# A retention layer and its mixture of adapters: scores between transposes, an interleaved tail, adapter weights from another queue

## The chip, the cores and the metric

The kernel runs on one core of a Trainium2 chip. The metric is the device time of one execution in microseconds (us); the median of three runs of the kernel before is 203.73 us (203.21 to 206.26). The engines are TensorE (PE; its weight loads are PEld), VectorE (DVE), ScalarE (ACT), GpSimd (POOL) and SyncE (SP), which here only issues transfers. Each engine works through its own list of instructions in order and waits on semaphores for the others. Transfers issued by any of them are moved by the core's 16 DMA engines.

## The reference

```python
# q, k, v: 8 batches x 8 heads x 576 positions x 64, float32
scores = q @ k.T / sqrt(64)
ret = (scores * gamma[h] ** (i - j) where i >= j, else 0) @ v
x = ret.transpose(0, 2, 1, 3).reshape(8 * 576, 512)      # 4608 tokens
logits = x @ w_gate                                      # 8 experts
w = softmax over the two largest logits of each token
out = x + sum over those two experts of w * ((x @ A[e]) @ B[e])   # rank 16
```

## The kernel before

**Tiling.** The 576 positions are four chunks of 128 and a tail of 64. The eight batches are two quads of four. A *unit* is one chunk and two batches of a quad: 16 full units, numbered 0 to 15, and after them two tail units, 16 and 17, each with four batches of 64 positions. Loads are made by chunk and quad: q, k and v are 1 MB each for a full chunk (`issue`, line 165), and three buffers of each are kept. A loop over the units (line 521) calls the stages in an order written out by hand; `mm`, `vec` and `act` (lines 80 to 87) chain the instructions of PE, DVE and ACT in exactly the order of the calls. GpSimd's and SyncE's instructions are not chained: a scheduler places them, from its own estimate of when their data will be there.

**Stages of a unit t.** `stage_T` transposes q and k on PE into PSUM (`pqT`, `pkT`), from where ACT copies them to `qT` and `kT`. `stage_S` computes scores (`ps`, in the tail `pe`) for its two batches; DVE multiplies them with the triangular mask into `rt` (`rh`). `stage_Q` adds the product of q and the running state `P` (`px`), `stage_U` computes the update of the state (`pu`, then `pn` on DVE and `P` on GpSimd), `stage_R` adds the product of masked scores and v to `px`, which DVE scales into `xT`. `stage_Z` multiplies `xT` with the adapter and gate weights (`AW`, result `pz`) and takes the two largest logits; `stage_W` makes the gate on ACT (`sg`) and DVE (`cm`) and scales the low-rank product (`zc`). `stage_B` transposes `xT` back into `po`, `stage_X` transposes `zc` (`pzt`, copied to `zT`), `stage_Y` adds the product of `zT` and `Bcat` to `po`, has ACT copy it to `osb`, and issues the stores. Stages W, B, X and Y of a unit run during the next one. All PSUM tiles share eight buffers (`pp`).

**The start.** Units 0 and 1 go through T, S, Q, U, R and Z together at t = 0, with idle matmuls (`spin`) ahead of each operand's first transposes. v must be scaled by GpSimd (`scale_v`, line 214) before pu and px may read it, in place, two instructions a unit. The adapter weights are four transfers of 64 KB and the gate weights one of 16 KB, all from SyncE (`load_moe`, line 150), between the loads of the first and of the second quad; GpSimd then copies `AW[0]` to `AW[1]` with the halves of the partitions exchanged (line 537).

**The tail.** Unit 16 takes batches 0 to 3 and unit 17 batches 4 to 7; their loads are issued apart, each with two halves per operand. The stores of a tail unit are four of 64 rows.

Of the kernel before, what the change touches and what calls it, by code (L numbers as in the profile page):

```python
# [10 lines left out]
FP32 = mybir.dt.float32  # L11
# [7 lines left out]
def kernel(  # L19
# [129 lines left out]

    def load_moe():  # L150
        for dt in range(HP):
            nc.sync.dma_start(
                out=AW[0][:, dt, 0:ER].rearrange("p (e r) -> p e r", e=E),
                in_=moe_A[:, 128 * dt : 128 * dt + 128, :].rearrange("e d r -> d e r"),
            )
        nc.sync.dma_start(
            out=AW[0][:, :, ER : ER + E],
            in_=moe_w_gate.rearrange("(t p) e -> p t e", p=128),
        )
        nc.gpsimd.dma_start(out=Bcat, in_=moe_B.rearrange("e r d -> (e r) d"))  # L160


    nat = {}

    def issue(n):
        if n >= len(quads):
            return
        c, qd = quads[n]
        first = n == 0
        tl = [  # L170
            iop.tile([128, QUAD, H, Dh], FP32, tag=tag, name=tag) for tag in ("q32", "k32", "v32")
        ]
        if c == NFULL:
            for src, dst in zip((q, k, v), tl):
                for g in range(2):
                    nc.sync.dma_start(
                        out=dst[64 * g : 64 * g + 64, 0:2].rearrange("p s h d -> p (s h) d"),
                        in_=src[
                            QUAD * qd + 2 * g : QUAD * qd + 2 * g + 2, :, C * c : C * c + L, :
                        ].rearrange("s h j d -> j (s h) d"),  # L180
                    )
        def load(n, lo, hi):
            nc.sync.dma_start(  # L183
                out=tl[n][:, lo:hi].rearrange("p b h d -> p (b h) d"),
                in_=(q, k, v)[n][
                    QUAD * qd + lo : QUAD * qd + hi, :, C * c : C * c + C, :
                ].rearrange("b h j d -> j (b h) d"),
            )

        if first:  # L190
            for n in range(3):
                load(n, 0, 4)
                if n == 1:
                    nc.sync.dma_start(out=pack, in_=dr_pack.ap())  # L194
            load_moe()
        elif c < NFULL:
            for n in range(3):
                load(n, 0, 4)
        for sl in range(2):
            nat[(c, qd, sl)] = [x[:, 2 * sl : 2 * sl + 2] for x in tl]  # L200
# [20 lines left out]
                op=ALU.mult,  # L221
            )

    def stage_T(t, pause=0):

        q32, k32, v32 = nat[units[t]]
        s = st.setdefault(t, {})
        for src, nm in ((q32, "qT"), (k32, "kT")):
            if nm == "kT":
                spin(pause)  # L230
            dst = s[nm] = wk.tile([128, 2, HP, C], FP32, tag=nm, name=nm)
            ps = [pp.tile([128, HP, 2, L], FP32, tag="pb", name=f"p{nm}") for _ in range(2)]
            for hp in range(HP):
# [20 lines left out]
    def stage_Q(t):  # L254
# [8 lines left out]
        for hp in range(HP):  # L263
            for y in range(1 if full else 2):
                for ho in range(2):
                    for x in range(2):
                        Pt = P[2 * qd + sl][:, :, x] if full else P[2 * qd + x][:, :, y]
                        i = slice(0, C) if full else rows(y)
                        mm(
                            px[x][rows(ho ^ x), hp, i],  # L270
                            lhsT=Pt[rows(ho), hp, :],
                            rhs=s["qT"][rows(ho), x, hp, i],
                            start=(hp == 0 and y == 0),
                            stop=False,
                            skip_group_check=True,
                        )

    def stage_S(t):
        s = st[t]
        rt = s.setdefault("rt", {})  # L280
        if not is_full(t):
# [20 lines left out]
                )  # L302
                rt[ho] = r
            return
        for b in range(2):
            ps = [pp.tile([128, HP, C], FP32, tag="pb", name=f"ps{ho}") for ho in range(2)]
            for hp in range(HP):
                for ho in range(2):
# [102 lines left out]
                    )  # L411
        s["po"] = po

    def stage_X(t):
        s = st[t]
        pzt = pp.tile([128, 2, 128], FP16, tag="pb", name="pzt")
        for g in range(2):
            mm(
                pzt[:, g, :], lhsT=s["zc"][:, g, :], rhs=ident16,
                is_transpose=True, start=True, stop=True,  # L420
            )
        zt = mo.tile([128, 2, 128], FP16, tag="zT", name="zT")
        act("copy", out=zt, in_=pzt)
        s["zT"] = zt

    def stage_Z(t):
        s = st[t]
        pz = pp.tile([128, 2, ER + E], FP32, tag="pb", name="pz")
        for g in range(2):
            for dt in range(HP):  # L430
                mm(
                    pz[:, g, :],
                    lhsT=s["xT"][g][:, dt, :],
                    rhs=AW[g][:, dt, :],
                    start=(dt == 0),
                    stop=(dt == HP - 1),
                    skip_group_check=True,
                )
        m8 = mo.tile([128, 2, E], FP32, tag="m8", name="m8")
        ns = mo.tile([128, 2], FP32, tag="ns", name="ns")  # L440
        sg = mo.tile([128, 2, E], FP32, tag="sg", name="sg")
        cm = mo.tile([128, 2, E], FP32, tag="cm", name="cm")
        lg = mo.tile([128, 2, E], FP32, tag="lg", name="lg")
        vec("tensor_copy", out=lg, in_=pz[:, :, ER : ER + E])
        for g in range(2):
            vec("max", out=m8[:, g, :], in_=lg[:, g, :])
        vec("scalar_tensor_tensor", 
            out=ns, in0=m8[:, :, 0], scalar=-1.0, in1=m8[:, :, 1],
            op0=ALU.mult, op1=ALU.subtract,
        )  # L450
        s["route"] = lg, m8, ns, sg, cm, pz

    def stage_W(t):
        s = st[t]
        lg, m8, ns, sg, cm, pz = s.pop("route")
        for g in range(2):
            act("activation", 
                out=sg[:, g, :], in_=lg[:, g, :], func=AFT.Sigmoid,
                bias=ns[:, g : g + 1], scale=2.0,
            )  # L460
        for g in range(2):
            vec("scalar_tensor_tensor", 
                out=cm[:, g, :], in0=lg[:, g, :], scalar=m8[:, g, 1:2], in1=sg[:, g, :],
                op0=ALU.is_ge, op1=ALU.mult,
            )
        zc = mo.tile([128, 2, ER], FP16, tag="zc", name="zc")
        for g in range(2):
            vec("tensor_tensor", 
                out=zc[:, g, :].rearrange("p (e r) -> p e r", e=E),
                in0=pz[:, g, 0:ER].rearrange("p (e r) -> p e r", e=E),  # L470
                in1=cm[:, g, :].unsqueeze(2).broadcast_to((128, E, R)),
                op=ALU.mult,
            )
        s["zc"] = zc

    def stage_Y(t):
        c, qd, sl = units[t]
        s = st.pop(t)
        po = s["po"]
        osb = outp.tile([128, 2, HP, 2, Dh], FP32, tag="osb", name="osb")  # L480
        bv = Bcat.rearrange("p (a o d) -> p a o d", a=HP, o=2)
        for cc in range(2):
            for g in range(2):
                mm(
                    po[cc][:, g, :, :],
                    lhsT=s["zT"][:, g, :],
                    rhs=bv[:, :, cc ^ g, :],
                    start=False,
                    stop=True,
                    skip_group_check=True,  # L490
                )
        for cc in range(2):
            for g in range(2):
                act("copy", out=osb[:, g, :, cc ^ g, :], in_=po[cc][:, g])
        of = osb.rearrange("p g a o d -> p g (a o d)")
        for g in range(2):
            for x in range(1 if c < NFULL else 2):
                bt = 2 * sl + g if c < NFULL else 2 * g + x
                n0 = S * (QUAD * qd + bt) + C * c
                if c < NFULL:  # L500
                    nc.sync.dma_start(out=out[n0 : n0 + C, :], in_=of[:, g, :])
                else:
                    nc.sync.dma_start(out=out[n0 : n0 + L, :], in_=of[rows(x), g, :])

    issue(0)
    issue(1)
# [14 lines left out]
    for t in range(NU):  # L521
# [3 lines left out]
            scale_v(t + 1)  # L525
        if t == 0:
            spin(12)
            stage_T(0, pause=12)
            stage_T(1)
            stage_S(0)  # L530
            stage_S(1)
            for u in range(2):
# [2 lines left out]
                stage_R(u)  # L535
            for ho in range(2):
                gp.tensor_copy(out=AW[1][rows(ho)], in_=AW[0][rows(1 - ho)])
            for u in range(2):
                stage_Z(u)
            stage_T(2)  # L540
            continue
        if t == 1:
            continue
        done = [0, 1] if t == 2 else [t - 1] if t > 2 else []
        if not is_full(t):
            stage_Q(t)
        stage_S(t)
        for u in done:
            stage_W(u)
        if t + 1 < NU:  # L550
            stage_T(t + 1)
        for u in done:
            stage_B(u)
        if is_full(t):
            stage_Q(t)
        stage_U(t)
        stage_R(t)
        for u in done:
            stage_X(u)
        stage_Z(t)  # L560
        for u in done:
            stage_Y(u)
    stage_W(NU - 1)
    stage_B(NU - 1)
    stage_X(NU - 1)
    stage_Y(NU - 1)
    return

# [28 lines left out]
```

## Time and profile before

| | |
|---|---|
| median of three runs | 203.73 us |
| the profiled execution | 203.81 us |
| its span, first to last instruction | 202.1 us |
| PE busy | 184.5 us, 91% of the span |
| DVE, ACT, POOL busy | 109.4, 71.5, 58.3 us |
| bytes moved | 38.73 MB, mean 192 GB/s |

Times inside the span count from its first instruction. Busy time of PE is that of matmuls which overlap each other, so it tells where PE had work, not how near it is to its peak. A line of the timeline reads: start, length, engine, line of the kernel, operation, output and inputs, shapes, number of instructions, and in brackets how long the engine stood idle before and what released it. PE, DVE and ACT instructions bear the line of the helper that records them (81, 84, 87), so they are told apart by their tiles.

### The profile page before, as it was taken

To read this page: it belongs to the slowest core of one execution; us is meant where nothing else is said; L and a number is where in the kernel's file an instruction comes from. 1 tells how busy PE (TensorE), PEld (TensorE's weight loads), DVE (VectorE), ACT (ScalarE), POOL (GpSimd) and SP (SyncE) were. 2 spreads that over 40 slices of the span, in tenths; PEclk is the share of its full clock that TensorE was granted. 3 is DMA by queue.
4 is the path that set the end of the run, shared out by engine and by line. 5 is a ranking of instruction groups with operands and counts; after the bars stand their busy time and mean duration, and the time that the engine had idled before them with its cause. 6 is when DMAs were issued, how large, how long until landed. Compare 5 with 4: busy or idle time off the path is not lost.

```text
span 202.1 us, 8056 instructions
## 1 busy us (share of the span) xinstructions
PE 184.5 (91%) x3588; PEld 164.6 (81%) x3588; DVE 109.4 (54%) x270; ACT 71.5 (35%) x196; POOL 58.3 (29%) x68
## 2 busy tenths in 40 slices
PE   7889977999999999999999999899999999989740
PEld 2378966899999999999999999799999999978620
DVE  0249628648647565757555655646464646363420
ACT  2040054163525252525243434234343434343060
POOL 5059108043046203636203722610502060200000
PEclk9999999999999999999999999999999999999995
DMA  4996999999999949952989798439145702022044
GB/s 122 312 241 90 296 275 246 284 276 254 322 310 270 289 175 272 274 181 109 250 245 303 247 257 267 111 88 255 51 135 122 194 11 100 3 107 99 11 104 104
DMA packets 47698, 38.73 MB, mean 192 GB/s; under 512 B 18352, under 2 KB 43056, under 8 KB 47664
## 3 DMA queue, kind: packets, MB, share of 16 engines
q1 hardware_dynamic: 47520, 38.09, 66.0%
q8 instruction: 28, 0.46, 1.0%
q0 software_dynamic: 144, 0.13, 0.4%
q14 instruction: 6, 0.05, 0.1%
HBM read 28.91 MB, written 9.44 MB: 190 GB/s over the span
## 4 chain that ended last, share of the span: by engine, by line
PE 79%; DVE 7%; SPq 4%; DMA 3%; ACT 2%; POOL 1%; issue 1%; ACTq 0%; POOLq 0%
PE px L81 22%; PE pz L81 17%; PE ps L81 13%; PE po L81 9%; PE pu L81 9%; PE pkT L81 3%; PE pqT L81 3%; DMA v<-in_v_dram 3%; DVE rt L84 2%; SPq L183 2%; DVE cm L84 2%; SPq L194 2%; PE pzt L81 2%; POOL v L217 1%; ACT osb L87 1%
## 5 line engine op out<-in xcount | busy, mean ns | idle before, releaser
L84 DVE TENSOR_TENSOR rt<-ps,tri 128x512 f32<-128x512 f32 x64 | 39.6, 682 | 13.4 <-PE ps L81 13.4
L217 POOL TENSOR_TENSOR v<-v,pack 128x512 f32<-128x512 f32 x36 | 36.5, 1043 | 23.7 <-DMA v<-in_v_dram 23.7
L349 POOL TENSOR_TENSOR P<-pn,gdec 128x512 f32<-128x512 f32 x12 | 15.3, 1273 | 82.2 <-DVE pn L84 82.2
L81 PE MATMUL pz<-AW,xT 128*128 128x136 f32 x288 | 37.2, 283 | 1.1 <-DVE xT L84 1.1
L81 PEld LDWEIGHTS pz<-AW,xT 128*128 128x128 f32 x288 | 34.5, 190 | 1.6 <-DVE xT L84 1.6
L81 PE MATMUL ps<-qT,kT 64*128 64x128 f32 x512 | 32.6, 278 | 1.6 <-ACT kT L87 1.4
L81 PEld LDWEIGHTS ps<-qT,kT 64*128 64x128 f32 x512 | 29.7, 188 | 4.6 <-PE po L81 2.7
L87 ACT COPY osb<-po 128x256 f32<-128x256 f32 x72 | 21.5, 389 | 30.0 <-PE po L81 28.2
L81 PE MATMUL px<-rt,v 128*64 128x128 f32 x512 | 30.8, 273 | 0.0
L84 DVE TENSOR_TENSOR xT<-px,asc 128x512 f32<-128x512 f32 x36 | 24.7, 691 | 7.3 <-PE px L81 6.0
L87 ACT COPY qT<-pqT 128x512 f32<-128x512 f32 x32 | 17.2, 590 | 31.3 <-PE pqT L81 31.3
L81 PEld LDWEIGHTS px<-rt,v 128*64 128x64 f32 x512 | 27.8, 137 | 0.0
L87 ACT COPY zT<-pzt 128x256 f16<-128x256 f16 x18 | 6.6, 373 | 53.8 <-PE pzt L81 53.8
L87 ACT COPY kT<-pkT 128x512 f32<-128x512 f32 x36 | 19.6, 608 | 9.7 <-PE pkT L81 9.7
L81 PE MATMUL pu<-v,k 128*64 128x64 f32 x512 | 18.6, 225 | 1.4 <-DVE zc L84 1.0
L81 PEld LDWEIGHTS pu<-v,k 128*64 128x64 f32 x512 | 16.4, 138 | 3.9 <-issue 3.1
L84 DVE TENSOR_TENSOR pn<-pu,P 128x512 f32<-128x512 f32 x12 | 8.3, 691 | 20.4 <-PE pu L81 20.4
L81 PE MATMUL po<-id,xT 64*128 64x64 f32 x288 | 15.7, 229 | 2.2 <-DVE zc L84 1.6
L84 DVE COPY lg<-pz 128x16 f32<-128x16 f32 x18 | 3.1, 174 | 25.8 <-PE pz L81 25.8
L81 PEld LDWEIGHTS po<-id,xT 64*128 64x128 f32 x288 | 12.1, 139 | 4.4 <-DVE rt L84 2.4
L81 PE MATMUL px<-qT,P 64*64 64x128 f32 (+1 forms) x512 | 15.6, 262 | 0.0
L81 PEld LDWEIGHTS px<-qT,P 64*64 64x64 f32 x512 | 12.5, 133 | 1.3 <-issue 0.4
(42 smaller groups left out, 147.3 us busy)
## 6 DMA issues: line engine op xcount, KB each, us to landing
out_dram<-osb SPq DMA_DIRECT2D x32, 256.0 KB, 3.3
q<-in_q_dram SPq DMA_DIRECT2D x4, 256.0 KB, 4.4
k<-in_k_dram SPq DMA_DIRECT2D x4, 256.0 KB, 3.7
v<-in_v_dram SPq DMA_DIRECT2D x4, 256.0 KB, 4.0
out_dram<-osb SPq DMA_DIRECT2D x8, 128.0 KB, 2.3
AW<-in_moe_A_dram SPq DMA_DIRECT2D x4, 64.0 KB, 3.5
q<-in_q_dram SPq DMA_DIRECT2D x8, 0.2 KB, 6.3
k<-in_k_dram SPq DMA_DIRECT2D x8, 0.2 KB, 9.1
```

The costliest lines, as they stand in the source:

```text
L81: chain("pe", nc.tensor.matmul(*args, **kw))
L84: chain("dve", getattr(nc.vector, fn)(**kw))
L87: chain("act", getattr(nc.scalar, fn)(**kw))
L183: nc.sync.dma_start(out=tl[n][:, lo:hi].rearrange("p b h d -> p (b h) d"), in_=(q, k, v)[n][QUAD * qd + lo : QUAD * qd + hi, :, C * c : C ...
L194: nc.sync.dma_start(out=pack, in_=dr_pack.ap())
L217: nc.gpsimd.tensor_tensor(out=vv[:, b], in0=vv[:, b], in1=gv[:, 0 if is_full(t) else 1].unsqueeze(2).broadcast_to((128, H, Dh)), op=ALU.mult,)
L349: nc.gpsimd.tensor_tensor(out=Pt, in0=pn, in1=gdec, op=ALU.mult)
```

## The change

- In the loop over full units, the scores of the first batch come first, then the transposes of the next unit's q, then the scores of the second batch, then the transposes of k. The gate's sigmoid is a stage of its own (`stage_V`), called between the first scores and q's transposes.
- Of units 0 and 1, both q are transposed ahead of both k, with 10 instead of 12 idle matmuls between. Unit 0's W, B, X and Y move into t = 0.
- `load_moe` issues its five transfers from ScalarE's queue, after the copies of unit 0's kT; the transfer of `Bcat` stays on GpSimd's.
- Units 16 and 17 are interleaved: 17's state product, scores and products with v are placed among the routing stages of 16, and 17 itself routes and stores its two halves one after the other. The second PSUM tile of those halves is copied out by DVE.
- A tail unit takes two batches of each quad; both units' tail loads are issued together, as six transfers of 512 KB instead of twelve of 256 KB, and a tail store is one of two batches of 64 rows.

The stages X, Z, W and Y take the halves to work on as an argument `gs`; their instructions for a whole unit are the same as before. In the built program, the order of GpSimd's first instructions after `asc` is: the two copies of AW, then the scaling of v. SyncE's first loads are q, k, the constants, v, and then at once q, k and v of the second and third quads.

```diff
     def load_moe():
         for dt in range(HP):
-            nc.sync.dma_start(
+            act(
+                "dma_start",
                 out=AW[0][:, dt, 0:ER].rearrange("p (e r) -> p e r", e=E),
                 in_=moe_A[:, 128 * dt : 128 * dt + 128, :].rearrange("e d r -> d e r"),
             )
...
         if c == NFULL:
+            if qd > 0:
+                return
             for src, dst in zip((q, k, v), tl):
                 for g in range(2):
                     nc.sync.dma_start(
-                        out=dst[64 * g : 64 * g + 64, 0:2].rearrange("p s h d -> p (s h) d"),
-                        in_=src[
-                            QUAD * qd + 2 * g : QUAD * qd + 2 * g + 2, :, C * c : C * c + L, :
-                        ].rearrange("s h j d -> j (s h) d"),
+                        out=dst[64 * g : 64 * g + 64].rearrange("p s h d -> p (s h) d"),
+                        in_=src[HALF * g : HALF * g + HALF, :, C * c : C * c + L, :].rearrange(
+                            "s h j d -> j (s h) d"
+                        ),
                     )
...
         for cc in range(2):
-            for g in range(2):
-                act("copy", out=osb[:, g, :, cc ^ g, :], in_=po[cc][:, g])
+            for g in gs:
+                if spread and cc == 1:
+                    vec("tensor_copy", out=osb[:, g, :, cc ^ g, :], in_=po[cc][:, g])
+                else:
+                    act("copy", out=osb[:, g, :, cc ^ g, :], in_=po[cc][:, g])
...
+            bt = HALF * g + 2 * qd
+            nc.sync.dma_start(
+                out=out.rearrange("(b s) d -> b s d", b=B)[bt : bt + 2, C * c : C * c + L, :],
+                in_=of[:, g, :],
+            )
...
         if t == 0:
             spin(12)
-            stage_T(0, pause=12)
-            stage_T(1)
+            stage_T(0, ("qT",))
+            stage_T(1, ("qT",))
+            spin(10)
+            stage_T(0, ("kT",))
+            load_moe()
+            stage_T(1, ("kT",))
             stage_S(0)
             stage_S(1)
...
-            for u in range(2):
-                stage_Z(u)
-            stage_T(2)
+            stage_Z(0)
+            stage_W(0)
+            stage_T(2, ("qT",))
+            stage_Z(1)
+            stage_T(2, ("kT",))
+            stage_B(0)
+            stage_X(0)
+            stage_Y(0)
             continue
...
+        if t == NU - 1:
+            break
+        if is_full(t):
+            stage_S(t, (0,))
+            stage_V(t - 1)
+            stage_T(t + 1, ("qT",))
+            stage_S(t, (1,))
+            stage_W(t - 1)
+            stage_T(t + 1, ("kT",))
+            stage_B(t - 1)
+            stage_Q(t)
+            stage_U(t)
+            stage_R(t)
+            stage_X(t - 1)
+            stage_Z(t)
+            stage_Y(t - 1)
+            continue
+
+        stage_Q(t)
         stage_S(t)
+        stage_W(t - 1)
+        stage_T(t + 1)
+        stage_B(t - 1)
         stage_R(t)
+        stage_Q(t + 1)
+        stage_X(t - 1)
         stage_Z(t)
+        stage_W(t)
+        stage_Y(t - 1)
+        stage_S(t + 1)
+        stage_B(t)
+        stage_X(t)
+        stage_R(t + 1)
+        stage_Y(t)
+        for g in range(2):
+            stage_Z(t + 1, (g,))
+            stage_W(t + 1, (g,))
+        stage_B(t + 1)
+        for g in range(2):
+            stage_X(t + 1, (g,))
+            stage_Y(t + 1, (g,), spread=True)
```

More of the change, by code (lines that the diff above doesn't have):

```diff
@@ L155, in load_moe @@
             )
-        nc.sync.dma_start(
+        act(
+            "dma_start",
             out=AW[0][:, :, ER : ER + E],
@@ L163 @@
     nat = {}
+    HALF = B // 2
+    assert HALF == QUAD
     def issue(n):
@@ L176, in issue @@
                     nc.sync.dma_start(
-                        out=dst[64 * g : 64 * g + 64, 0:2].rearrange("p s h d -> p (s h) d"),
-                        in_=src[
-                            QUAD * qd + 2 * g : QUAD * qd + 2 * g + 2, :, C * c : C * c + L, :
-                        ].rearrange("s h j d -> j (s h) d"),
-                    )
+                        out=dst[64 * g : 64 * g + 64].rearrange("p s h d -> p (s h) d"),
+                        in_=src[HALF * g : HALF * g + HALF, :, C * c : C * c + L, :].rearrange(
+                            "s h j d -> j (s h) d"
+                        ),
+                    )
+            for u in range(2):
+                nat[(c, u, 0)] = [x[:, 2 * u : 2 * u + 2] for x in tl]
+            return
         def load(n, lo, hi):
@@ L194, in issue @@
                     nc.sync.dma_start(out=pack, in_=dr_pack.ap())
-            load_moe()
         elif c < NFULL:
@@ L222, in scale_v, with stage_T @@
             )
-    def stage_T(t, pause=0):
-        q32, k32, v32 = nat[units[t]]
+    def stage_T(t, names=("qT", "kT")):
         s = st.setdefault(t, {})
-        for src, nm in ((q32, "qT"), (k32, "kT")):
-            if nm == "kT":
-                spin(pause)
+        for nm in names:
+            src = nat[units[t]][0 if nm == "qT" else 1]
             dst = s[nm] = wk.tile([128, 2, HP, C], FP32, tag=nm, name=nm)
@@ L266, in stage_Q @@
                     for x in range(2):
-                        Pt = P[2 * qd + sl][:, :, x] if full else P[2 * qd + x][:, :, y]
+                        Pt = P[2 * qd + sl][:, :, x] if full else P[2 * x + qd][:, :, y]
                         i = slice(0, C) if full else rows(y)
@@ L276, in stage_Q, with stage_S @@
                         )
-    def stage_S(t):
+    def stage_S(t, bs=(0, 1)):
         s = st[t]
@@ L304, in stage_S @@
             return
-        for b in range(2):
+        for b in bs:
             ps = [pp.tile([128, HP, C], FP32, tag="pb", name=f"ps{ho}") for ho in range(2)]
@@ L412, in stage_B, with stage_X, stage_Z @@
         s["po"] = po
-    def stage_X(t):
+    BOTH = (0, 1)
+    def stage_X(t, gs=BOTH):
         s = st[t]
-        pzt = pp.tile([128, 2, 128], FP16, tag="pb", name="pzt")
-        for g in range(2):
+        n = len(gs)
+        pzt = pp.tile([128, n, 128], FP16, tag="pb", name="pzt")
+        for y, g in enumerate(gs):
             mm(
-                pzt[:, g, :], lhsT=s["zc"][:, g, :], rhs=ident16,
+                pzt[:, y, :], lhsT=s["zc"][g], rhs=ident16,
                 is_transpose=True, start=True, stop=True,
             )
-        zt = mo.tile([128, 2, 128], FP16, tag="zT", name="zT")
+        zt = mo.tile([128, n, 128], FP16, tag=f"zT{n}", name="zT")
         act("copy", out=zt, in_=pzt)
-        s["zT"] = zt
-    def stage_Z(t):
+        for y, g in enumerate(gs):
+            s.setdefault("zT", {})[g] = zt[:, y, :]
+    def stage_Z(t, gs=BOTH):
         s = st[t]
-        pz = pp.tile([128, 2, ER + E], FP32, tag="pb", name="pz")
-        for g in range(2):
+        n = len(gs)
+        pz = pp.tile([128, n, ER + E], FP32, tag="pb", name="pz")
+        for y, g in enumerate(gs):
             for dt in range(HP):
                 mm(
-                    pz[:, g, :],
+                    pz[:, y, :],
                     lhsT=s["xT"][g][:, dt, :],
@@ L438, in stage_Z @@
                 )
[L439 to L443, printed above, removed]
+        m8 = mo.tile([128, n, E], FP32, tag=f"m8{n}", name="m8")
+        ns = mo.tile([128, n], FP32, tag=f"ns{n}", name="ns")
+        lg = mo.tile([128, n, E], FP32, tag=f"lg{n}", name="lg")
         vec("tensor_copy", out=lg, in_=pz[:, :, ER : ER + E])
-        for g in range(2):
-            vec("max", out=m8[:, g, :], in_=lg[:, g, :])
-        vec("scalar_tensor_tensor",
+        for y in range(n):
+            vec("max", out=m8[:, y, :], in_=lg[:, y, :])
+        vec(
+            "scalar_tensor_tensor",
             out=ns, in0=m8[:, :, 0], scalar=-1.0, in1=m8[:, :, 1],
@@ L450, in stage_Z, with stage_V @@
         )
-        s["route"] = lg, m8, ns, sg, cm, pz
-    def stage_W(t):
+        s[("route", gs)] = lg, m8, ns, pz
+    def stage_V(t, gs=BOTH):
         s = st[t]
[L455 to L459, printed above, removed]
-            )
-        for g in range(2):
-            vec("scalar_tensor_tensor",
-                out=cm[:, g, :], in0=lg[:, g, :], scalar=m8[:, g, 1:2], in1=sg[:, g, :],
+        n = len(gs)
+        lg, m8, ns, pz = s[("route", gs)]
+        sg = mo.tile([128, n, E], FP32, tag=f"sg{n}", name="sg")
+        for y in range(n):
+            act(
+                "activation",
+                out=sg[:, y, :], in_=lg[:, y, :], func=AFT.Sigmoid,
+                bias=ns[:, y : y + 1], scale=2.0,
+            )
+        s[("route", gs)] += (sg,)
@@ L464, in stage_W @@
+    def stage_W(t, gs=BOTH):
+        s = st[t]
+        n = len(gs)
+        if len(s[("route", gs)]) == 4:
+            stage_V(t, gs)
+        lg, m8, ns, pz, sg = s.pop(("route", gs))
+        cm = mo.tile([128, n, E], FP32, tag=f"cm{n}", name="cm")
+        zc = mo.tile([128, n, ER], FP16, tag=f"zc{n}", name="zc")
+        for y in range(n):
+            vec(
+                "scalar_tensor_tensor",
+                out=cm[:, y, :], in0=lg[:, y, :], scalar=m8[:, y, 1:2], in1=sg[:, y, :],
                 op0=ALU.is_ge, op1=ALU.mult,
@@ L465, in stage_W @@
             )
[L466 to L471, printed above, removed]
+        for y, g in enumerate(gs):
+            vec(
+                "tensor_tensor",
+                out=zc[:, y, :].rearrange("p (e r) -> p e r", e=E),
+                in0=pz[:, y, 0:ER].rearrange("p (e r) -> p e r", e=E),
+                in1=cm[:, y, :].unsqueeze(2).broadcast_to((128, E, R)),
@@ L472, in stage_W, with stage_Y @@
                 op=ALU.mult,
             )
-        s["zc"] = zc
-    def stage_Y(t):
+            s.setdefault("zc", {})[g] = zc[:, y, :]
+    def stage_Y(t, gs=BOTH, spread=False):
         c, qd, sl = units[t]
-        s = st.pop(t)
+        s = st[t]
         po = s["po"]
-        osb = outp.tile([128, 2, HP, 2, Dh], FP32, tag="osb", name="osb")
+        if gs[0] == 0:
+            s["osb"] = outp.tile([128, 2, HP, 2, Dh], FP32, tag="osb", name="osb")
+        osb = s["osb"]
         bv = Bcat.rearrange("p (a o d) -> p a o d", a=HP, o=2)
@@ L482, in stage_Y @@
         for cc in range(2):
-            for g in range(2):
+            for g in gs:
                 mm(
                     po[cc][:, g, :, :],
-                    lhsT=s["zT"][:, g, :],
+                    lhsT=s["zT"][g],
                     rhs=bv[:, :, cc ^ g, :],
@@ L492, in stage_Y @@
         for cc in range(2):
-            for g in range(2):
-                act("copy", out=osb[:, g, :, cc ^ g, :], in_=po[cc][:, g])
-        of = osb.rearrange("p g a o d -> p g (a o d)")
[L496 to L503, printed above, removed]
+            for g in gs:
+                if spread and cc == 1:
+                    vec("tensor_copy", out=osb[:, g, :, cc ^ g, :], in_=po[cc][:, g])
+                else:
+                    act("copy", out=osb[:, g, :, cc ^ g, :], in_=po[cc][:, g])
+        of = osb.rearrange("p g a o d -> p g (a o d)")
+        for g in gs:
+            if c < NFULL:
+                n0 = S * (QUAD * qd + 2 * sl + g) + C * c
+                nc.sync.dma_start(out=out[n0 : n0 + C, :], in_=of[:, g, :])
+                continue
[4 more added lines that the diff above has]
+            )
     issue(0)
@@ L543 @@
             continue
-        done = [0, 1] if t == 2 else [t - 1] if t > 2 else []
-        if not is_full(t):
-            stage_Q(t)
-        stage_S(t)
[L548 to L556, printed above, removed]
+        if t == NU - 1:
[8 more added lines that the diff above has]
+            stage_B(t - 1)
+            stage_Q(t)
+            stage_U(t)
[3 more added lines that the diff above has]
+            stage_Y(t - 1)
+            continue
+        stage_Q(t)
+        stage_S(t)
+        stage_W(t - 1)
+        stage_T(t + 1)
+        stage_B(t - 1)
         stage_R(t)
-        for u in done:
-            stage_X(u)
+        stage_Q(t + 1)
+        stage_X(t - 1)
         stage_Z(t)
[L561 to L566, printed above, removed]
+        stage_W(t)
[12 more added lines that the diff above has]
+            stage_Y(t + 1, (g,), spread=True)
     return
```

## The prediction

> **What bounds the kernel now.** I read the page's totals first, then the chain that ended last, then the start of the run on GpSimd and SyncE, then the stores.
>
> ```profile
> span 202.1 us, 8056 instructions
> PE 184.5 (91%) x3588; PEld 164.6 (81%) x3588; DVE 109.4 (54%) x270; ACT 71.5 (35%) x196; POOL 58.3 (29%) x68
> PE   7889977999999999999999999899999999989740
> ```
>
> TensorE is the bound: its row is at 9 from the eighth slice to almost the end. A full unit repeats every 10.2 us (scores start at 72.10, 82.30, 92.50) with no gap, so an exchange inside that loop moves little. Only the two ends have room. The chain:
>
> ```profile
> 15.57 2.06 POOL v L217 x2
> 17.67 1.04 PE pu L81 x28
> ...
> 28.67 1.10 ACT kT L87 x2
> ...
> 33.49 1.87 DVE cm L84 x2
> ...
> 42.47 1.99 PE ps L81 x32
> ```
>
> The reader is to see that GpSimd's scaling of v releases the first pu, that two later waits (for kT and for cm) cost some 3 us, and that unit 3's scores start at 42.47. I measure the start of the run by that moment. GpSimd and SyncE in order of time:
>
> ```profile
> 15.57 4.05 POOL L217 TENSOR_TENSOR v<-v,pack 128x512 f32<-128x512 f32 x4 [1.15 <-DMA v<-in_v_dram]
> 19.68 1.32 POOL L537 COPY AW<-AW 64x544 f32<-64x544 f32 x2
> ...
> 10.18 6.37 SPq L152 DMA_DIRECT2D AW<-in_moe_A_dram  x4
> 16.60 0.59 SPq L156 DMA_DIRECT2D AW<-in_moe_w_gate_dram  x1
> ```
>
> GpSimd scales v first and copies the adapter weights (AW) second. The end:
>
> ```profile
> 194.38 0.43 PE L81 MATMUL pzt<-ident,zc 128*128 128x128 f16 x2 [1.32 <-DVE zc L84]
> ...
> 195.80 1.20 ACT L87 COPY osb<-po 128x256 f32<-128x256 f32 x4 [0.53 <-PE po L81]
> ...
> out_dram<-osb SPq DMA_DIRECT2D x32, 256.0 KB, 3.3
> out_dram<-osb SPq DMA_DIRECT2D x8, 128.0 KB, 2.3
> ```
>
> The last matmul ends at 195.9, the last copy at 197.0, the last store lands near 200.9, and 1.2 us later the span ends.
>
> **What the Trainium skill says.** (1) "DMA: Bandwidth & Descriptors", section Queues, rings and completion order: each DMA engine serves the queues in turn and switches only at a packet's end. The trace agrees, and shows how long a turn is. Bcat (GpSimd's queue, issued at 2.72) began on each engine only when that engine had finished its whole share of the 1 MB q load (ends 6.08 to 6.64), although k, issued at 2.21, was waiting too; k followed. A turn was a whole transfer. (2) The same page, section Why a DMA increments its semaphore by 16 and not by 1: a transfer runs on the largest number of engines, at most 16, that divides the outermost dimension of both sides; a smaller number takes the lowest-numbered engines. Every store of before has 128 or 64 there. While stores run, some 95 packets of 2 KB start per 0.5 us at 84 ns each: 95 x 84 = 8.0 us of work in 0.5 us, 16 engines. A smaller number is in no trace of before. (3) "TensorE: Matmul & The Clock Gate", Part 1: after some 3.4 us without work the clock halves until it has been busy as long. The trace agrees: the first twelve spin matmuls took 5.30 us, the second twelve 2.76, and the clock is 0.50 from 199 us on. (4) "SBUF — State Buffer", section Who interferes with whom: a VectorE instruction with two SBUF inputs waits for a GpSimd instruction that reads SBUF. Agreed: a pair of cm takes 0.35 us alone and 1.95 at 33.41, inside GpSimd's scaling.
>
> **The change part by part.** In the built order of the changed kernel GpSimd's two AW copies stand *ahead* of the first scaling of v. So the first pu waits until all five AW transfers have landed.
>
> *When AW lands.* The issues stand on ScalarE behind the first two kT copies, which end at 12.00 + 2.09/2 = 13.05. Before, a first packet followed an issue by some 1.4 us (q: 17.39 to 18.8), so AW is ready near 14.5, as v ends on the engines (14.5 to 15.2). SyncE now goes straight to the next q, k and v. By packets: an AW transfer is 64 per engine at 11 ns, 0.7 us; a load is 64 at 54 ns, 3.5 us; the gate weights 32 at 9 ns, 0.3. One turn each: AW 15.6, q 19.1, AW 19.8, k 23.3, AW 24.0, v 27.5, AW 28.2, next q 31.7, gate 32.0, landed about 33. The bounds are 19 (where it landed before, issued from SyncE alone) and 36 (first turn missed). I take 33.
>
> *What follows.* AW copies 1.32 to 34.3; two scalings 2.06 to 36.4; the rest of pu 1.0 to 37.4. TensorE then runs px, pu, px (1.75 + 0.93 + 1.75 = 4.4) to 41.8; both pz 3.9, unit 2's transposes 1.1, po 0.7, pzt 0.1, Bcat product 0.45, together 6.3, to 48.1; unit 2's own round 9.1 (10.2 less 1.03, as chunk 0 has no state product) to 57.2. Against 42.47: +14.7. That has already taken out the waits for kT and cm. TensorE stands idle from about 19 to 35, so it restarts at half clock: between 0 and 3.3 us (the first spins lost 5.30 - 2.76 = 2.5); I take 2.0. **Start: +16.7.**
>
> *ScalarE's issues.* Five at 0.58 to 0.72 are 3.0 us, up to the 7.0 that SyncE spent; queued behind are unit 1's kT copies (1.05), and behind those its scores (1.92), ready at 19.0 to 23.0. The late pu hides it; without that cover it costs 2 to 6.
>
> *The loop.* Scores, qT, scores, kT are the same 64 matmuls in another order, and DVE's order is unchanged. rt of the second batch comes 0.5 us later, hidden by the state product and pu (2.1 us). Sigmoid already ran ahead of cm on ScalarE. Zero, within 1 us either way: the wait of 0.98 at 128.88 may shift, as cm meets a scaling there. The tail loads become six of 512 KB, issued in the same place, and their four scalings stand behind the ninth P update, before 157; covered by 20 us, and 4 us if not.
>
> *The tail.* From unit 16 on TensorE has 15.5 us of work and took 20.7 (175.2 to 195.9), 5.2 in waits. Now the next state product (1.05) lies over the wait for xT (0.6), and unit 17's scores, po and px over routing. I follow it: scores of 17 to 185.35, po and pzt to 186.3, px waits for rh until 187.25 and ends 188.5, two half pz to 191.1, routing of the halves done 191.6 and 193.0, last product 194.1, last half copied 194.5 on two engines. That is 2.5 earlier. With a store of 3.3 us issued at 194.6, and 1.2 behind, the end would be 199.1: -3.0.
>
> *But the stores.* The four tail stores now have a DRAM side of 2 x 64 x 512 against 128 rows. By (2) they get two engines, the same two each time: 128 packets over 2 are 64, at 84 ns 5.4 us, and four in a row 21.5. The first is issued at 190.2, starts a microsecond later (before: 193.23 to 194.0), so the data end at 191.2 + 21.5 = 212.7; 0.4 to land, 1.2 to finish: 214.3. **Tail: +12.2** instead of -3.0. The lower bound of this cost is zero, should the sides be cut alike.
>
> *Sum* against the profiled execution's 203.81 (span 202.1 and 1.7 around it): 203.8 + 16.7 + 12.2 = 232.7. The median, 203.73, stands 0.1 below it, so **232.6**.
>
> **The rivals.**
> - *The weights go together.* At the first end of a load every waiting AW transfer passes: AW 15.6, q 19.1, the rest 2.4, landed 22. The chain is 11 shorter: +3.7, clock 1.8, start +5.5. Bcat was a single transfer and can't exclude it. With narrow stores 221.4; if AW landed by 20, some 218.
> - *The stores stay wide* (the change doesn't narrow what it seems to). Tail -3.0, start +16.7: 217.4. The descriptor generator might cut both sides alike; the skill's rule speaks against it.
> - *Not slower: the filled tail pays.* Place: from 175 on; price -3.0; it decides if the stores stay wide and the start costs less than 7, which needs AW to land by about 23. With AW at 19 to 22 it gives 202 to 206. For it: 5.2 us of tail waits. Against: whole-transfer turns.
>
> **How the numbers follow.** Forecast 0.44 (228 to 237, by AW at 31 to 36 and the clock's 0 to 3.3); weights together with narrow stores 0.22, with AW by 20 another 0.08; wide stores with late weights 0.15; not slower 0.11. From 215 to 237 all but the last and the edges are in, about 0.8. Slower by over 2%, which is about what a measurement of this kernel can tell from no change, has 0.89, within it 0.09, faster 0.02.
>
> **What would show it.** Right: AW's copies on GpSimd near 33 and ahead of the scaling; a hole on TensorE from 19 to 35 with a low clock; unit 3's scores near 59; last copy some 2.5 earlier counted from there; four stores of over 5 us each, and 20 us of DMA at a small share with every engine idle. Wrong: AW landed by 23, or tail stores landing in 3 us; either takes 11 to 15 us out.

## The result, and the profile after

The changed kernel takes **220.54 us** (median; 219.94 to 222.28), the kernel before on the same chip 204.13: ratio 1.0802, 95% interval [1.0696, 1.0907]. The profiled execution took 219.94 us with a span of 218.2, against 202.1 before. Ratios in this document compare executions in the chip's faster state alone, while medians take all of them; of the six of e4 below three were slower, so its median (201.34) lies 1.8 us above that of the other three (199.5). The page's totals, and from the rows of 40 slices TensorE, its granted clock and the transfers:

```profile
span 218.2 us, 8025 instructions
PE 183.8 (84%) x3586; PEld 165.3 (76%) x3586; DVE 110.8 (51%) x274; ACT 72.8 (33%) x195; POOL 58.2 (27%) x68
...
PE   7860689899999999999999999999999999981000
...
PEclk9995569999999999999999999999999999999555
DMA  4999989289849929882989669999320202021111
```

TensorE does as much work as before (183.8 us against 184.5). What is new is at the two ends: an empty slice and a low clock in the fourth to sixth, and three slices at the end in which only the transfers do something, at a tenth.

**The start.** GpSimd in order of time:

```profile
24.92 1.31 POOL L573 COPY AW<-AW 64x544 f32<-64x544 f32 x2 [10.78 <-DMA AW<-in_moe_w_gate_dram]
26.31 8.05 POOL L226 TENSOR_TENSOR v<-v,pack 128x512 f32<-128x512 f32 x8
```

The copies of AW do stand ahead of the scaling of v, and GpSimd stood idle for 10.78 us until the gate weights had landed. ScalarE (ACTq are its issues, ACT its own work):

```profile
12.24 4.99 ACTq L87 DMA_DIRECT2D AW<-in_moe_A_dram  x3
17.27 3.28 ACTq L87 DMA_DIRECT2D AW<-in_moe_w_gate_dram  x1
20.59 1.07 ACT L87 COPY kT<-pkT 128x512 f32<-128x512 f32 x2 [7.77 <-issue]
```

With the first of the five (0.41 at 11.79) the issues took 8.7 us, and unit 1's kT copies waited behind them. TensorE:

```profile
21.72 3.79 PE L81 MATMUL ps<-qT,kT 64*128 64x128 f32 x32 [6.78 <-ACT kT L87]
...
27.41 0.48 PE L81 MATMUL pu<-v,k 128*64 128x64 f32 x4 [1.90 <-POOL v L226]
...
51.40 1.16 PE L81 MATMUL ps<-qT,kT 64*128 64x128 f32 x16
...
93.11 0.67 PE L81 MATMUL po<-id,xT 64*128 64x64 f32 x16
...
100.14 1.05 PE L81 MATMUL ps<-qT,kT 64*128 64x128 f32 x14
```

Unit 1's scores wait 6.78 us for kT and then run at half clock (3.79 us instead of some 1.9; the clock was 0.5 from 17.3 to 31.0). pu waits 1.90 more for v. Unit 3's scores start at 51.40, **8.9 us later** than before (42.47 by the chain; the timeline, where matmuls overlap, has 42.40).

**The loop** gains. A unit begins at 90.18 and the next at 100.14: 9.96 us, against 10.20. In before, the same transposes of xT took longer, and TensorE's waits name the reason. First the timeline, then the waits, of the kernel before:

```profile
85.11 0.95 PE L81 MATMUL po<-id,xT 64*128 64x64 f32 x16
```

```profile
PEld po L81 <- DVE rt L84: 2.4, 13, 0.5
```

(2.4 us in total, 13 times, the longest 0.5.) In the changed kernel this wait is gone, and the block takes 0.67. From unit 3's scores to unit 16's state product it is 128.36 us (51.40 to 179.76) against 132.76: **4.4 us less**.

**The tail.** From unit 16's state product to the end of the last copy to `osb` it is 19.0 us (to 198.77) against 21.8: **2.8 less**. But from that copy to the end of the span it is 19.4 us against 5.1: **14.3 more**. A stretch of that time (columns: stretch, length, busy time of PE, PEld, DVE, ACT, POOL, granted clock, share of the DMA engines, GB/s):

```profile
205.00:210.00 5.00, 0.00 (x0) 0.00 (x0) 0.00 (x0) 0.00 (x0) 0.00 (x0) 0.50 0.13 51
```

No engine does anything, and the share of 0.13 is two of 16 DMA engines (2/16 = 0.125). The data run from 195.0 to 217.0, and the stores end at 201.6, 206.7, 211.9 and 217.0: the first takes 6.6 us, each of the others 5.1.

8.9 - 4.4 - 2.8 + 14.3 = 16.0; the spans differ by 16.1.

### The profile page after: what moved, and what is told of

Same layout as the page of the kernel before. It is cut to its first block, busy times and chain, and to the rows that moved or that the text cites. A ratio compares the mean times of both kernels' runs of the same rounds, so it can differ in the third digit from the quotient of the medians.

```text
span 218.2 us, 8025 instructions
## 1 busy us (share of the span) xinstructions
PE 183.8 (84%) x3586; PEld 165.3 (76%) x3586; DVE 110.8 (51%) x274; ACT 72.8 (33%) x195; POOL 58.2 (27%) x68
## 5 line engine op out<-in xcount | busy, mean ns | idle before, releaser
L84 DVE TENSOR_TENSOR rt<-ps,tri 128x512 f32<-128x512 f32 x64 | 41.1, 686 | 23.9 <-PE ps L81 20.1
L81 PE MATMUL ps<-qT,kT 64*128 64x128 f32 x512 | 37.6, 291 | 7.4 <-ACT kT L87 7.4
L81 PEld LDWEIGHTS ps<-qT,kT 64*128 64x128 f32 x512 | 32.6, 197 | 10.7 <-ACT kT L87 7.8
L87 ACT COPY kT<-pkT 128x512 f32<-128x512 f32 x36 | 19.3, 590 | 23.6 <-PE pkT L81 15.8
L87 ACT COPY zT<-pzt 128x256 f16<-128x256 f16 (+1 forms) x19 | 6.9, 361 | 48.5 <-PE pzt L81 48.5
L81 PE MATMUL pu<-v,k 128*64 128x64 f32 x512 | 19.5, 231 | 2.4 <-POOL v L226 2.4
L81 PEld LDWEIGHTS pu<-v,k 128*64 128x64 f32 x512 | 17.1, 143 | 5.1 <-POOL v L226 2.9
L87 ACT ACTIVATE sg<-lg,ns 128x8 f32<-128x8 f32 x36 | 9.3, 315 | 20.5 <-DVE ns L84 20.5
L84 DVE COPY lg<-pz 128x16 f32<-128x16 f32 (+1 forms) x19 | 3.3, 173 | 24.5 <-PE pz L81 24.5
L81 PE MATMUL po<-Bcat,zT 128*128 128x256 f16 x72 | 11.0, 273 | 1.9 <-ACT zT L87 1.9
```

What stands on the lines that cost most here:

```text
L81: chain("pe", nc.tensor.matmul(*args, **kw))
L84: chain("dve", getattr(nc.vector, fn)(**kw))
L87: chain("act", getattr(nc.scalar, fn)(**kw))
```

## The experiments

My theory: two things make the kernel slower, the four tail stores on two DMA engines and the adapter weights from ScalarE's queue; the rest of the change gains. The rivals: that one of the two is all of the loss; that in the start only GpSimd's order matters; that the gain of the loop comes from elsewhere. Each ratio is to the kernel before on the same chip (205.10 us in the first four, 205.58 in the last four). Differences between these runs are given by medians; by ratios they come out within 0.4 us of these, but for e4 against e8, where both are given. The changed kernel was timed apart, against 204.13 for the kernel before, so differences to it are less certain: both figures are given.

| run | what differs | us | ratio to before, interval |
|---|---|---|---|
| e1_wide_stores | tail stores of 64 rows | 207.63 | 1.0123 [1.0042, 1.0203] |
| e2_weights_from_sync | weights from SyncE | 209.84 | 1.0236 [1.0170, 1.0302] |
| e3_both | both of these | 195.61 | 0.9525 [0.9463, 0.9588] |
| e4_loop_alone | before, with the loop's new order only | 201.34 | 0.9737 [0.9660, 0.9815] |
| e5_v_first | e1, GpSimd scales v ahead of AW | 202.63 | 0.9880 [0.9817, 0.9944] |
| e6_v_first_late_issue | e5, weights issued after all kT copies | 198.89 | 0.9696 [0.9633, 0.9760] |
| e7_one_narrow | e3 with the last store narrow | 200.85 | 0.9797 [0.9736, 0.9858] |
| e8_tail_in_series | e3, units 16 and 17 in series | 198.16 | 0.9657 [0.9603, 0.9711] |

**Wide stores.**

```diff
-            nc.sync.dma_start(
-                out=out.rearrange("(b s) d -> b s d", b=B)[bt : bt + 2, C * c : C * c + L, :],
-                in_=of[:, g, :],
-            )
+            for y in range(2):
+                n0 = S * (bt + y) + C * c
+                nc.sync.dma_start(out=out[n0 : n0 + L, :], in_=of[rows(y), g, :])
```

> The changed kernel, with each tail store cut into two of 64 rows, as before; all else kept. Theory (a store with two batches outermost runs on two DMA engines): the stores after the last copy take 4 to 5 us instead of 19.4, so the time falls by some 15 to 16, to about 205. Rival (the long end is the landing of the last stores behind a slow queue, whatever their form): it stays near 220.

12.9 us come back (220.54 to 207.63; 13.9 by the ratios). From the end of the last copy to the end of the span it is 4.4 us (201.40 to 205.8) instead of 19.4. The same bytes in eight transfers instead of four are faster, here in a stretch of e1 with the columns as above:

```profile
203.00:204.00 1.00, 0.00 (x0) 0.00 (x0) 0.00 (x0) 0.00 (x0) 0.00 (x0) 0.50 0.88 203
```

I had expected 15 to 16. The end is 15.0 shorter, but in the profiled execution of e1 unit 3's scores come 2.6 us later (54.04), and its first kT copy 2.0 later (13.72 against 11.75), before anything that the edit touches.

**Weights from SyncE.** The stores stay narrow.

```diff
     def load_moe():
         for dt in range(HP):
-            act(
-                "dma_start",
+            nc.sync.dma_start(
```

`load_moe()` is called between the loads of the first and second quads again, as in before.

> The changed kernel, with the five weight transfers issued from SyncE between the loads of the first and second quad, as before; narrow tail stores kept. Theory (ScalarE's queue costs the start): unit 3's scores start at 40 to 42.5 instead of 51.4, GpSimd scales v ahead of the copies of AW, no stretch of half clock near 17 to 31, time 209 to 212. Rival (the start is late because the stages of unit 0 were pulled into it): unit 3's scores stay near 51 and the time near 220.

10.7 us come back (11.6 by the ratios), in the start. GpSimd now takes v first (its timeline in e2):

```profile
15.45 4.04 POOL L225 TENSOR_TENSOR v<-v,pack 128x512 f32<-128x512 f32 x4 [1.67 <-DMA v<-in_v_dram]
19.55 1.31 POOL L571 COPY AW<-AW 64x544 f32<-64x544 f32 x2
```

Nothing in the source asks for this order: the scheduler places GpSimd's instructions by when it thinks their data will land, so moving the issues reordered another engine. Their queue and their place among the calls moved together; which of the two changes the order was not tried. Unit 3's scores start at 40.22.

**Both.** The two diffs together.

> Both repairs in one: weights from SyncE and tail stores of 64 rows. Theory: the two costs add up, 220.5 - 15.5 - 10.3 = 194 to 196, below the kernel before by the loop (some 3 to 4 us), the tail (2.8) and two waits at the start (up to 3). Rival (the gain in the loop is only the loads being ahead after a late start): 198 to 200.

**195.61 us**, 4.75% below the kernel before, [4.1, 5.4] from the interval above: this version beats both kernels. Together the two edits bring 24.9, alone 12.9 + 10.7 = 23.6 (by the ratios 26.2 and 25.5): they add up within about 1 us, as two ends of a run should.

**The loop's order alone**, in the kernel before:

```diff
         if not is_full(t):
             stage_Q(t)
-        stage_S(t)
-        for u in done:
-            stage_W(u)
-        if t + 1 < NU:
-            stage_T(t + 1)
+            stage_S(t)
+            ...
+        else:
+            stage_S(t, (0,))
+            stage_T(t + 1, names=("qT",))
+            stage_S(t, (1,))
+            for u in done:
+                stage_W(u)
+            stage_T(t + 1, names=("kT",))
```

> The kernel before, with only the order in the loop over full units changed: first batch's scores, q's transposes, second batch's scores, then routing, k's transposes. Theory (po no longer waits for a PSUM buffer that the masking of the second batch frees): a full unit takes 9.95 us instead of 10.2, the time falls by 3 to 4 to about 200.5. Rival (the shorter unit comes from loads that are further ahead): a unit stays at 10.2 and the time at 204.

2.6% faster by the ratio, [1.9, 3.4], which is 5.4 us of 205.1; the medians differ by 3.8, and the spans of the profiled executions by 4.8 (202.1 to 197.3). TensorE's timeline in e4:

```profile
91.20 1.16 PE L81 MATMUL ps<-qT,kT 64*128 64x128 f32 x16
...
94.13 0.67 PE L81 MATMUL po<-id,xT 64*128 64x64 f32 x16
...
101.16 0.37 PE L81 MATMUL ps<-qT,kT 64*128 64x128 f32 x1
```

A unit is 9.96 us, po takes 0.67, and the wait for rt is no longer among the waits. So the gain of a unit is the order's, and neither ScalarE's separate sigmoid stage nor the changed start is needed for it. Of the 4.8 in the spans, 3.3 lie between unit 3's scores and unit 16's state product (41.39 to 170.83), where the changed kernel gains 4.4; two early units take 9.50 and 10.45 us in e4 and 8.92 and 9.95 there, and why was not followed. DVE does not finish the masks sooner: counted from the unit's first scores, the last one ends at 3.93 us (95.13) against 3.68 in before. po simply no longer needs a buffer that a late mask must free. In before, its first matmul is at 85.11 and the rest go on at some 85.35, just after the third mask (84.6 to 85.3). In e4 all 16 run from 94.13, while DVE is still at the third mask. With q's transposes between the two scores, the eight PSUM buffers pass from tile to tile in another order; which tile hands over to which was inferred from the waits, not tried by itself.

**v ahead of AW.** e1, and on GpSimd the scalings for units 0 and 1 and the copies of AW are chained in the order of the calls. The weights still come from ScalarE's queue.

```diff
-            nc.gpsimd.tensor_tensor(
+            i = nc.gpsimd.tensor_tensor(
...
+            if t < 2:
+                chain("pool", i)
...
-                gp.tensor_copy(out=AW[1][rows(ho)], in_=AW[0][rows(1 - ho)])
+                chain("pool", gp.tensor_copy(out=AW[1][rows(ho)], in_=AW[0][rows(1 - ho)]))
```

> The changed kernel with 64-row tail stores, and on GpSimd v of units 0 and 1 scaled ahead of the copies of AW; the five transfers stay on ScalarE's queue. Theory: two things of the new queue cost time at the start, GpSimd's order and ScalarE's own issuing, which holds the kT copies to 20.6 us and with them the scores, at half clock. With the order alone mended the first scaling comes near 15.5 as before, but TensorE still idles for kT from 17 to 21, and pz waits for AW: unit 3's scores near 48 to 50 (51 to 54 with AW first, 40 to 41 with the weights from SyncE), the time 201 to 205. Rival: the order on GpSimd was all of the start's cost: unit 3's scores near 42, the time 195 to 197.

202.63, as the theory has it: order is 5.0 of the 12.0 us that lie between e1 and e3. The 5.0 include the clock, which in the start stood at half for 17.1 us of e1's profile and for 10.2 of e5's. v is scaled from 17.40 on, but it has nobody to serve yet (TensorE in e5):

```profile
23.46 3.78 PE L81 MATMUL ps<-qT,kT 64*128 64x128 f32 x32 [7.14 <-ACT kT L87]
27.17 1.96 PE L81 MATMUL pu<-v,k 128*64 128x64 f32 x32
```

The scores wait for kT, whose copies stand behind ScalarE's issues until 22.34, and both run at half clock.

**Issues after the kT copies.** e5 with one line moved:

```diff
             stage_T(0, ("kT",))
-            load_moe()
             stage_T(1, ("kT",))
+            load_moe()
```

> As the run before, with the five transfers issued by ScalarE after the kT copies of units 0 and 1 instead of between them. Theory: the scores no longer wait for ScalarE's issuing, AW lands within 2 us of where it did (24.5), since it waits for the turns of the load queue and not for its issue; then px and pz are what AW may hold. Unit 3's scores near 44 to 46, the time 197 to 200. Rival: the new place is too late for a turn, AW lands a whole load later (near 28), pz waits, and it is no faster than the run before.

3.7 us faster again (198.89). The scores run at 14.13 at full clock, and what waits is the product with AW itself (TensorE in e6):

```profile
26.56 1.17 PE L81 MATMUL pz<-AW,xT 128*128 128x136 f32 x8 [3.07 <-issue]
27.94 2.12 PE L81 MATMUL pz<-AW,xT 128*128 128x136 f32 x8 [0.22 <-POOL AW L574]
```

GpSimd's copies of AW start at 26.58; counted from the first kT copy, which moves by up to 2.3 us from one execution to another, that is 13.6 us, in e5 13.6 and in the changed kernel 13.2. A later issue did not land later: what AW waits for are the turns of the load queue. The remaining 3.3 us to e3 are about that wait (3.07 + 0.22; by the profiled spans 2.8). So the start's loss has three parts, by medians: GpSimd's order 5.0, ScalarE's blocked issues 3.7, the late landing 3.3; together the 12.0 between e1 and e3. The shares are for taking them off in this order; with AW still ahead of v, moving the issues alone was not run.

**One narrow store.** e3, with the last of the tail's stores as in the changed kernel:

```diff
+            if qd == 1 and g == 1:
+                nc.sync.dma_start(
+                    out=out.rearrange("(b s) d -> b s d", b=B)[bt : bt + 2, C * c : C * c + L, :],
+                    in_=of[:, g, :],
+                )
+                continue
```

> The changed kernel with the weights from SyncE and 64-row stores in the tail, except the last store, which has a DRAM side of 2 x 64 x 512. Theory: that store takes two engines and 5.1 to 5.4 us in place of some 2.3: 3 us more at the end of the span, the time 198 to 200 against 195.6. Rival: a single such store is spread over more engines when nothing else is in flight, and 195.6 stays.

200.85, 5.2 more than e3. The store takes two engines even with nothing else in flight (stretches of e7, columns as above):

```profile
194.00:195.00 1.00, 0.00 (x0) 0.00 (x0) 0.00 (x0) 0.00 (x0) 0.00 (x0) 0.50 0.13 25
...
197.00:198.00 1.00, 0.00 (x0) 0.00 (x0) 0.00 (x0) 0.00 (x0) 0.00 (x0) 0.50 0.13 51
198.00:199.00 1.00, 0.00 (x0) 0.00 (x0) 0.00 (x0) 0.00 (x0) 0.00 (x0) 0.50 0.13 51
```

Its data last from 192.8 to 199.1, in the first half slower than 51 GB/s. My expectation was 2 us too low: I set the 5.1 us of data against the 2.3 us from issue to landing of a wide store, most of which is latency that the narrow store has as well. In e3 the data end 2.9 us after the last copy, here 8.0.

**The tail in series.** e3, with the order of before for units 16 and 17; joined loads and wide stores stay.

```diff
+        for u in (t, t + 1):
+            stage_Q(u)
+            stage_S(u)
+            stage_W(u - 1)
+            if u == t:
+                stage_T(u + 1)
+            stage_B(u - 1)
+            stage_R(u)
+            stage_X(u - 1)
+            stage_Z(u)
+            stage_Y(u - 1)
+        stage_W(t + 1)
+        stage_B(t + 1)
+        stage_X(t + 1)
+        stage_Y(t + 1)
```

> The changed kernel with the weights from SyncE and 64-row tail stores, and with units 16 and 17 one after the other, in the order that the tail had before. Theory: the interleaving is worth 2.5 to 3 us, since the products of unit 17 fill waits for the routing of 16: 198.0 to 198.8 against 195.6, all of it after unit 16's state product. Rival: the shorter tail of the changed kernel comes from something else (loads joined, halves copied by two engines), and the time stays within 1 us of 195.6.

198.16, 2.55 above e3. From unit 16's state product to the end of the span it is 26.6 us (169.56 to 196.2) against 24.1. TensorE in e8:

```profile
188.53 0.43 PE L81 MATMUL pzt<-ident,zc 128*128 128x128 f16 x2 [1.32 <-DVE zc L84]
189.47 0.61 PE L81 MATMUL po<-Bcat,zT 128*128 128x256 f16 x4 [0.52 <-ACT zT L87]
```

The waits of before are back, with the same 1.32. Two things of the tail went together here, the interleaving and the halves of unit 17, whose second copies DVE makes. From the end of the last product to that of the last copy it is 1.1 us in e8 and 0.5 in e3, so some 0.6 of the 2.55 are the copies on two engines; the rest is the filled waits, of which the halves have a share that was not tried apart. In e3 the last products still wait 0.73 and 0.36 for zT.

**What is left over.** e8 has, beyond e4, only the new start and the joined tail loads. By ratios 1.6 us lie between them, by the profiled spans 1.1, of which 0.85 come before unit 3's scores (by medians 3.2, with e4's as said above). The intervals of the two overlap; that this part of the change gains at all is likely and not shown.

## Why the prediction was right or wrong

Slower, by 16 instead of 29 us; the direction held, and so did the two causes, AW ahead of v and the narrow stores. The 220.54 lies below the stated 228 to 237: two terms of the sum were off, the landing of AW and the loop. It comes close to the 221.4 of the rival in which the weights go together, and that is luck: that sum has AW at 22 and nothing for the loop, where AW landed at 24.5 and the loop gave back 4.4.

| term | predicted | measured in the trace | runs |
|---|---|---|---|
| start | +16.7 | +8.9 | weights -10.7 or -11.6 (e2), -12.0 (e1 to e3) |
| loop | 0, within 1 | -4.4 | -3.3 on the same stretch, -5.4 by the ratio of the whole run (e4) |
| tail without stores | -3.0 | -2.8 | -2.55 (e8 to e3) |
| stores | +15.2 | +14.3 | -12.9 or -13.9 (e1), -14.2 (e2 to e3) |

- **"One turn each" failed.** I let one AW transfer pass per turn of the load queue, and AW land at 33. A turn was a whole load, as taken: v, AW, q, AW, k, gate weights, v. But two AW transfers passed in a turn. The packets of ScalarE's queue come in three groups, from 14.7, 19.0 and 23.4 us, of 2080, 2080 and 528: two transfers of 1024 and 16 each, twice, and the gate weights (512 and 16). "DMA: Bandwidth & Descriptors", section Queues, rings and completion order, in the Trainium skill says that an engine goes round the queues packet by packet, at most 64 descriptors each. An AW transfer is 64 on each engine, so I read it as one per turn; the trace says two (in e6 first one, then two), and decides. AW landed at 24.5, 8.5 us early. The rival that all go together had it at 22, also not what happened: three turns were needed. Yet what passed at a turn was each time all that ScalarE had finished issuing. Its second issue was over at 12.84, the third only at 15.47, after the first group had begun; the fourth at 17.23, the gate weights' at 20.55, after the second. The same holds at all turns of e1, e5 and e6. So a rule of two per turn is not shown: all that waits may pass, and the issues that stood would then have kept the number at two. What makes an issue stand stays open.
- **The chain from there held.** I took 26.2 us from landing to unit 3's scores (33 to 57.2, and 2.0 for the clock); it was 26.9. With the true landing the same working gives +8.2, against 8.9.
- **"The late pu hides" ScalarE's issues: right, with the size off.** 8.7 us instead of 3 to 7; the scores ended at 25.5 and pu waited for v until 27.4. Without the cover I priced them at 2 to 6, and e5 against e6 shows 3.7. Being that long, they moved TensorE's hole: it lay ahead of unit 1's scores, from 14.9 to 21.7, and not between 19 and 35.
- **The clock.** Half speed as predicted, from 17.3. In the chain behind pu it cost some 1.2 us (pu 1.76 instead of 1.04, px 2.41 instead of 1.92), where I took 2.0; the rest fell on the scores. It halved 2.4 us after the last matmul (14.93 to 17.31), sooner than the 3.4 that I had taken; at the end it took 3.3 (198.31 to 201.63), and in before 2.0 (195.94 to 197.97).
- **"The loop: zero" failed.** I compared the number of matmuls and DVE's order and missed a wait that the profile before shows, that of po for rt, some 0.2 us in each of 13 units, because it is small in each and sits between busy stretches. The 0.98 at 128.88, which I had left within 1 us either way, did not come back either; 13 units by 0.25 and the 0.98 are 4.2 of the 4.4. An order of stages, by what the waits suggest, also decides which tile frees which PSUM buffer.
- **The tail** came out as followed: 2.8 of 3.0.
- **The stores**: two engines, as worked out from the shape; 5.1 us for each but the first, against 5.4, and 22.0 us from first data to last against 21.5.

## What to carry to other kernels

Look at the DRAM side's outermost dimension before joining two stores into one: 2 x 64 x 512 in place of two of 64 rows cost 5 us for a single store that nothing covered, and 13 to 14 for four in a row. Moving an issue to another engine's queue has three prices to be worked out apart, the landing between the turns of the other queue, the time for which the issuing engine stands still with all that is queued behind it, and what a scheduler does with the order on the engines that use the data. And a loop that shows TensorE busy throughout can still give 2.6%: read the waits of a tenth or two of a microsecond that recur in every unit.

## What the runs showed of the hardware that I had not expected

- While SyncE's loads were in flight, an issue on ScalarE could stand for several microseconds: 0.41, 0.60, 2.59, 1.74 and 3.28 us for the five in the changed kernel. In e6 it was 0.43, 0.64, 0.87, 4.19 and 1.10: from the third or the fourth on, an issue stood. SyncE's own 1 MB loads took 2.9 to 4.6 in the same time.
- ScalarE's queue, waiting for SyncE's 1 MB transfers, got one or two transfers through at each boundary, in four runs each time those whose issue was over by then.
- Narrow stores in a row did not spread out: four used two engines for 22.0 us, one alone for 6.4.
- The granted clock kept a value for a multiple of 3.41 us: in the changed kernel 10.24 at full, 13.65 at half and 170.67 at full, which are 3, 4 and 50 of them.
